# Half sequences 5 and 7 of a fused attention and FFN kernel: three rounds of scores in one burst, their fourth round in the next one's first burst, and later steps in a new order

## The chip, the cores and the metric

The kernel runs on one core of one Trainium2 chip. The metric is the device time of one execution in microseconds (us). Three runs of the kernel before took 229.24, 229.81 and 229.96 us; their median is 229.81. The profile is of one further execution.

## What is computed

An attention over 4 batches, 8 heads, 768 positions and 64 values per head is followed by an FFN over all 3072 tokens. Heads 0, 2 and 6 see every earlier position ("retrieval"); the other five see the first 4 positions and the last 64. The reference, cut:

```python
scores = scale * np.matmul(q, k.transpose(0, 1, 3, 2))
causal = rel >= 0
stream_keep = causal & (is_sink | in_win)          # 4 sinks, window of 64
mask = np.where(retr, causal, stream_keep)         # per head
a = softmax(np.where(mask, scores, -1e9))
x = np.matmul(a, v).transpose(0, 2, 1, 3).reshape(B * S, H * D)    # 3072 x 512
h = x @ w_in                                       # 512 -> 2048
g = h * (1.0 / (1.0 + np.exp(-beta * h)))
out = g @ w_out                                    # 2048 -> 512
```

## The kernel before

The 3072 tokens are eight *half sequences* (units) n = 0 to 7 of 384 queries: n = 2b + u is half u of batch b. The title counts them from one, so its fifth and seventh are n = 4 and n = 6, first halves. For each unit the kernel does, in this order:

- load q, k and v from HBM on the queue of the SP engine (`wf`), cast q and k to bf16 on GpSimd (`c`), and turn them with DMA transposes into `QK` (SP's queue too);
- copy pieces that the matmuls want side by side: `KP` and `QD` (the latter written into `k2f`), and for the values `vs`, `vz`, `VE` (from `vf`) beside `vb`;
- scores, on TensorE, in *rounds*: round (pi, ri) is round ri of head pair pi. A round writes one double bank of PSUM (`sp`, there are two) or, if `lent` says so, two of the four single banks (`b`). Rounds stand together in *bursts* (`BURSTS`, chosen by `kind_of(n)`). The exponentials of a round (`exps`, ScalarE, into `es`) free its banks, then its masks follow on VectorE;
- `pv`: exponentials times values into `sp`, and the sums of the exponentials into a bank; the sums go over `sc`, `rec` and `rd` (DMAs of a few KB and a reciprocal) and come back spread over the partitions as `R`; VectorE multiplies `sp` by `R` into `xT`, the FFN's input, and this frees `sp`;
- the FFN: 16 steps of four 128x384 matmuls with `w_in`, a tanh each on ScalarE (`t`) and the gate product on VectorE (`gT`); then 48 matmuls of 128x512 with `w_out` (in steps of three), a copy `osb` and a store.

TensorE (PE) works on 128x128 tiles in the FFN, on 64x64 or 64x128 tiles in the scores, 128x64 in `pv` and 128x32 in the sums. While one unit's FFN runs, the next units' attention stands between its steps.

Nothing is scheduled when it runs. Each step is declared with its engine or engines, what it needs and gives, and the buffers it takes and drops. The list `SEQUENCE` then says in which order all 1109 steps are written out, `CHOICE` the engine of those that may stand on several, and `SLOTS` the bank for each step that takes one. Every engine executes its own steps in that order. All instructions go through one recording helper, so that they all carry line L123.

In the scores of n = 4 and 6 the matmuls of a burst are handed out in turn to four 64x64 quadrants of the array (`scores_mixed`), which then work side by side.

Of the kernel before, what the change touches and what calls it, by code (L numbers as in the profile page):

```python
# [20 lines left out]
W = 64  # L21
# [71 lines left out]
]  # L93
CHOICE = (
    "daagaddadadddadaddaddgggdgdddgaaaggggggaaagdddaddaddagddddgaaddgddaaadagddadadagggggadggagdgggagggdd"
    "gaadaaadaaadaaadaadaadaaaada"
# [3 lines left out]
    "0301100101201013021302130210130211031001201032100123012301230123001200131230120130123012310021013203"  # L100
    "01130012103210013201320132100023102301231212310231001230123012301230210"
# [71 lines left out]
def kernel(  # L173
# [478 lines left out]
    def wide(pi, ri, n):  # L652
# [13 lines left out]
    def lent(pi, ri, n):  # L666
        return packed(n) and n % 2 and (pi, ri) in LENT
# [20 lines left out]
    def scores(x, pi, ri, mixed=None):  # L688
# [22 lines left out]
        for i, half in enumerate(rounds[ri]):  # L711
# [8 lines left out]
            for (kind, h, kb, col, q0, n) in half:  # L720
# [22 lines left out]
                else:  # L743
# [5 lines left out]
                    m = W if pi == 3 or (packed(x.n) and (ri > 1 or not u)) or ri == 4 else 128  # L749
# [722 lines left out]
```

## Time and profile before

| | |
|---|---|
| median of three runs | 229.81 us (229.24 to 229.96) |
| the profiled execution | 228.85 us |
| its span | 227.1 us |
| TensorE busy | 220.0 us, 2595 matmuls |
| VectorE busy | 152.0 us, 391 instructions |
| ScalarE busy | 144.4 us, 244 instructions |
| GpSimd busy | 97.1 us, 238 instructions |
| granted TensorE clock, mean | 0.999 |
| moved by DMA | 42.28 MB, mean 186 GB/s |

The span goes from the first to the last record of the trace; the time of the same execution holds 1.75 us more. Times of single instructions are from the profiled execution alone, which was 0.96 us shorter than the median. A matmul's length reaches into the next one in the rows, so distances between matmuls are taken from start to start.

### The profile page before, as it was taken

How to read it: one execution, taken by the hardware profiler on the slowest of the kernel's cores; microseconds unless marked ns; L12 is line 12 of the kernel's file. 1: busy time of each engine (PE TensorE's matmuls, PEld its weight loads, DVE VectorE, ACT ScalarE, POOL GpSimd, SP SyncE). 2: the span in 40 equal slices, each digit the busy share in tenths (PEclk: the TensorE clock that was granted, in tenths of full speed). 3: DMA queues.
4: the chain of work that ended last, by engine and by line, in shares of the span. 5: the costliest groups of instructions: out<-in, count | busy, mean ns of one | idle time of the engine just before them, and what ended most of it. 6: DMA issues, size and time to landing. Idle time of an engine off the chain costs nothing.

```text
span 227.1 us, 6564 instructions
## 1 busy us (share of the span) xinstructions
PE 220.0 (97%) x2595; PEld 127.2 (56%) x2595; DVE 152.0 (67%) x391; ACT 144.4 (64%) x244; POOL 97.1 (43%) x238
## 2 busy tenths in 40 slices
PE   7688999999999999999999999999999999999995
PEld 7564567664545565555654665465655555456543
DVE  5787988888292878856862668983796864157700
ACT  6899979886447488616786198318965665118620
POOL 5528966965978108749566293042800000000000
PEclk9999999999999999999999999999999999999999
DMA  6999999998999969999999996947801027021012
GB/s 185 283 321 369 242 343 349 371 335 217 233 205 244 213 131 235 270 176 208 267 219 189 202 214 192 219 26 178 188 0 46 4 89 200 3 92 46 3 46 92
DMA packets 84264, 42.28 MB, mean 186 GB/s; under 512 B 66042, under 2 KB 77002, under 8 KB 84234
## 3 DMA queue, kind: packets, MB, share of 16 engines
q1 hardware_dynamic: 83962, 41.67, 76.7%
q8 instruction: 20, 0.33, 0.6%
q10 hardware_dynamic: 272, 0.20, 0.3%
q14 instruction: 10, 0.08, 0.1%
HBM read 32.27 MB, written 6.37 MB: 170 GB/s over the span
## 4 chain that ended last, share of the span: by engine, by line
PE 87%; DMA 5%; DVE 3%; ACT 2%; SPq 1%; issue 1%; POOL 0%; ACTq 0%
PE b L123 77%; PE sp L123 10%; DMA vf<-in_v_dram 3%; DMA q2f<-in_q_dram 2%; DVE gT L123 1%; ACT t L123 1%; SPq L123 1%; ACT R L123 1%; DVE vs L123 1%; DVE xT L123 0%; ACT vb L123 0%; DVE QK L123 0%; POOL c L123 0%; DVE b L123 0%; DVE lo L123 0%
## 5 line engine op out<-in xcount | busy, mean ns | idle before, releaser
L123 PE MATMUL b<-xT,w_in 128*128 128x384 bf16 x512 | 89.9, 326 | 0.1
L123 PE MATMUL b<-w_out,gT 128*128 128x512 bf16 (+2 forms) x400 | 88.3, 371 | 0.0
L123 DVE SCALAR_TENSOR_TENSOR gT<-t,b 128x384 bf16<-128x384 f32 x128 | 68.5, 551 | 26.2 <-ACT t L123 22.5
L123 ACT ACTIVATE t<-b,beta_h 128x384 f32<-128x384 f32 x128 | 72.2, 586 | 18.3 <-PE b L123 9.7
L123 PEld LDWEIGHTS <-w_in 128*128 128x128 bf16 x512 | 48.6, 98 | 33.4 <-issue 0.6
L123 PEld LDWEIGHTS <-gT 128*128 128x128 bf16 x400 | 37.4, 98 | 40.9 <-issue 0.8
L123 ACT ACTIVATE es<-sp 128x1024 bf16<-128x1024 f32 (+2 forms) x44 | 41.2, 961 | 6.5 <-PE sp L123 6.0
L123 ACT ACTIVATE osb<-b 128x512 f32<-128x512 f32 (+1 forms) x18 | 10.5, 583 | 34.7 <-PE b L123 34.7
L123 DVE TENSOR_TENSOR xT<-sp,R 64x384 bf16<-64x384 f32 (+4 forms) x31 | 16.6, 554 | 12.2 <-PE sp L123 9.2
L123 POOL CAST c<-wf 128x256 bf16<-128x256 f32 x48 | 20.7, 473 | 7.6 <-DMA wf<-in_k_dram 7.4
L123 POOL COPY KP<-QK 128x24 bf16<-128x24 bf16 (+5 forms) x41 | 9.9, 286 | 27.1 <-DMA QK<-c 16.6
L123 PE MATMUL sp<-QK 64*64 64x128 bf16 (+6 forms) x360 | 14.9, 240 | 0.9 <-ACT QK L123 0.8
L123 DVE TENSOR_TENSOR es<-es,mask_s 128x128 bf16<-128x128 bf16 (+8 forms) x34 | 13.0, 402 | 3.8 <-ACT es L123 3.6
L123 PEld LDWEIGHTS <-QK 64*64 64x64 bf16 (+1 forms) x432 | 10.8, 106 | 7.2 <-issue 4.9
L123 DVE TENSOR_TENSOR es<-es,mask_c 128x128 bf16<-128x128 bf16 (+3 forms) x42 | 10.4, 272 | 6.2 <-ACT es L123 6.1
L123 POOL CAST vb<-wf 128x512 bf16<-128x512 f32 x18 | 11.2, 629 | 7.9 <-DMA wf<-in_v_dram 7.8
L123 PE MATMUL sp<-es,vb 128*64 128x64 bf16 (+5 forms) x245 | 13.0, 233 | 0.3 <-ACT es L123 0.3
L123 ACT COPY sc<-b 128x384 f32<-128x384 f32 x5 | 2.4, 479 | 15.7 <-PE b L123 15.7
L123 DVE TENSOR_SCALAR osb<-b 128x512 f32<-128x512 f32 (+1 forms) x7 | 4.7, 667 | 11.3 <-PE b L123 11.3
L123 PEld LDWEIGHTS <-vb 128*64 128x64 bf16 x257 | 11.6, 111 | 0.7 <-issue 0.3
L123 POOL CAST w_in<-wf 128x512 bf16<-128x512 f32 x16 | 9.4, 624 | 4.7 <-DMA wf<-in_moe_w_in_dram 4.6
L123 DVE COPY QK<-b 128x384 bf16<-128x384 bf16 (+1 forms) x13 | 8.2, 640 | 4.8 <-PE b L123 4.7
(120 smaller groups left out, 212.1 us busy)
## 6 DMA issues: line engine op xcount, KB each, us to landing
out_dram<-osb SPq DMA_DIRECT2D x23, 256.0 KB, 3.6
wf<-in_v_dram SPq DMA_DIRECT2D x18, 256.0 KB, 5.3
wf<-in_moe_w_in_dram SPq DMA_DIRECT2D x4, 1024.0 KB, 8.5
wf<-in_moe_w_out_dram SPq DMA_DIRECT2D x4, 1024.0 KB
R<-rd SPq DMA_DIRECT2D x9, 384.0 KB, 5.7
q2f<-in_q_dram SPq DMA_DIRECT2D x16, 192.0 KB, 4.1
wf<-in_q_dram SPq DMA_DIRECT2D x12, 256.0 KB, 4.0
wf<-in_k_dram SPq DMA_DIRECT2D x12, 256.0 KB, 3.8
```

What stands on the lines that cost most here:

```text
L123: ins = f(*a, **k)
```

## The change

For n = 4 and 6 the two bursts of two rounds become one burst of three rounds: (3,0), (0,0) and (0,1). Pair 3's rounds of these units write two single banks instead of a double bank. The round left over, (3,1), joins the first burst of the next unit (n = 5 and 7), which becomes (0,0), (0,1) and the other unit's (3,1). That burst is handed out to quadrants by `scores_mixed` as well, and its eight 64x128 matmuls are written as sixteen of 64x64. `scores_mixed` and the steps for exponentials and masks take the unit's number with each round.

There are two steps fewer, so every step behind them has a number that is lower by two. `SEQUENCE`, `CHOICE` and `SLOTS` are the same, but for these numbers, up to the first burst of n = 4. From there on the order, the banks, and the engine of some copies are new: the `vs` copies of n = 4 (two), one of n = 5 and one of n = 7, and the nine `KP` copies of n = 6 go from GpSimd to VectorE, one `vs` copy of n = 5 and one of n = 6 from VectorE to GpSimd, and eight output copies change between ScalarE and VectorE.

```diff
-    0, 2, 467, 477, 482, 478, 14, 12, 484, 4, 6, 483, 485, 8, 486, 464, 1, 3, 470, 80, 469, 28, 82, 26, 29, 27, 10,
...
+    0, 2, 465, 475, 480, 476, 14, 12, 482, 4, 6, 481, 483, 8, 484, 462, 1, 3, 468, 80, 467, 28, 82, 26, 29, 27, 10,
...
     BURSTS = [
         [[(0, 0), (0, 1)], [(3, 0), (3, 1)]],
         [[(0, 0), (0, 1)], [(1, 0), (0, 2), (3, 0)], [(2, 0), (0, 3), (3, 1)]],
-        [[(0, 0), (3, 0)], [(0, 1), (3, 1)]],
+        [[(3, 0), (0, 0), (0, 1)]],
     ]
 
     LENT = {(1, 0), (2, 0)}
 
     def lent(pi, ri, n):
+        if n in (4, 6):
+            return pi == 3
         return packed(n) and n % 2 and (pi, ri) in LENT
 
...
-                    m = W if pi == 3 or (packed(x.n) and (ri > 1 or not u)) or ri == 4 else 128
+                    m = W if pi == 3 or (packed(x.n) and (ri > 1 or not u or x.n > 4)) or ri == 4 else 128
...
-    def scores_mixed(x, bu):
+    def scores_mixed(bu):
 
         todo = []
-        for pi, ri in bu:
-            scores(x, pi, ri, todo)
+        for n, pi, ri in bu:
+            scores(units[n], pi, ri, todo)
...
-    BURST_COST = [[0.465, 0.48], [0.445, 0.7, 0.7], [0.465, 0.48]]
+    BURST_COST = [[0.465, 0.48], [0.445, 0.7, 0.7], [0.7]]
...
-        rounds = [(pi, ri) for bu in bursts for (pi, ri) in bu]
+        rounds = [(pi, ri) for bu in bursts for (pi, ri) in bu] + ([(3, 1)] if n in (4, 6) else [])
         for bi, bu in enumerate(bursts):
             needs, take, gives, drop, cost = [], [], [], [], 0.0
+            bu = [(n, pi, ri) for (pi, ri) in bu] + ([(n - 1, 3, 1)] if n in (5, 7) and not bi else [])
-            for (pi, ri) in bu:
+            for (m, pi, ri) in bu:
+                u, first_half = m % 2, m - m % 2
...
-                take += [("b", (n, pi, ri, i), 1) for i in range(2)] if lent(pi, ri, n) else [("sp", (n, pi, ri), 1)]
+                take += [("b", (m, pi, ri, i), 1) for i in range(2)] if lent(pi, ri, m) else [("sp", (m, pi, ri), 1)]
...
-            cost = cost if early else BURST_COST[kind_of(n)][bi]
+            cost = cost if early else 0.7 if len(bu) > 2 else BURST_COST[kind_of(n)][bi]
-            add("pe", cost, lambda bu=bu: scores_mixed(x, bu) if kind_of(n) == 2 else [scores(x, pi, ri) for (pi, ri) in bu],
+            add("pe", cost, lambda bu=bu: scores_mixed(bu) if kind_of(n) == 2 or any(w[0] != n for w in bu) else [scores(x, pi, ri) for (_, pi, ri) in bu],
...
-                add("act", exp_cost(pi, ri, n), lambda pi=pi, ri=ri: exps(x, pi, ri),
+                add("act", exp_cost(pi, ri, m), lambda m=m, pi=pi, ri=ri: exps(units[m], pi, ri),
-                    drop=[("b", (n, pi, ri, i)) for i in range(2)] if lent(pi, ri, n) else [("sp", (n, pi, ri))])
+                    drop=[("b", (m, pi, ri, i)) for i in range(2)] if lent(pi, ri, m) else [("sp", (m, pi, ri))])
```

The first place is TensorE ahead of the first burst of n = 5. In the rows, `w_out` and `w_in` are FFN matmuls, and `QK_109` is the transposed q and k of n = 5; brackets hold the semaphores that an instruction waits for. Before:

```order
L123 MATMUL b_2448<-w_out_125,gT 128x512
L123 LDWEIGHTS w_in_114 [waits DVE_49]
L123 MATMUL b_2462<-xT,w_in_114 128x384 [waits Activation_49]
L123 LDWEIGHTS w_in_114
L123 MATMUL b_2462<-xT,w_in_114 128x384 [waits DVE_49]
L123 LDWEIGHTS w_in_114
L123 MATMUL b_2462<-xT,w_in_114 128x384 [waits DVE_49]
L123 LDWEIGHTS w_in_114
L123 MATMUL b_2462<-xT,w_in_114 128x384 [waits DVE_49]
L123 LDWEIGHTS QK_109 [waits DMAHW7_49,DMAHW6_49,DMAHW5_49]
L123 MATMUL sp_2481<-QK_109 128x384 [waits PE_49]
```

After:

```order
L123 MATMUL b_2374<-w_out_124,gT 128x512
L123 LDWEIGHTS gT
L123 MATMUL b_2374<-w_out_125,gT 128x512
L123 LDWEIGHTS QK_109 [waits DMAHW6_49,DMAHW7_49,DMAHW5_49,DVE_49]
L123 MATMUL sp_2386<-QK_109 64x384 [waits PE_49]
L123 LDWEIGHTS QK_109
L123 MATMUL sp_2386<-QK_109 64x384
```

The step with `w_in` (four matmuls of n = 3) no longer stands between the `w_out` step and the burst, and the burst's first weight load waits for VectorE as well as for the three transposes. Further ahead, not shown, stand one burst of n = 4 where two were, and the sums of n = 3 have gone behind the burst.

The second place is SP's queue of DMAs ahead of the transposes `QK_109` of n = 5. `R`, `rd` and `q2f` belong to the sums of n = 3, `wf` with `in_k` is the load of n = 5's k, `vf` a small load of v for n = 4's `VE`, and `out` a store. Before:

```order
L123 DMA rd<-rec 96x32
L123 DMA wf<-in_k_dram 128x8x64 x3
L123 DMA out_dram<-osb 128x512 x2
L123 DMA R<-rd 64x2x384 x2
L123 DMA R<-rd 64x1536
L123 DMA q2f<-rd 64x128
L123 DMA vf<-in_v_dram 10x8x64 x3
L123 DMA_TRANSPOSE QK_109<-c 128x8x128 x3
```

After:

```order
L123 DMA out_dram<-osb 128x512
L123 DMA vf<-in_v_dram 10x8x64 x3
L123 DMA rd<-rec 96x32
L123 DMA wf<-in_k_dram 128x8x64 x3
L123 DMA R<-rd 64x2x384 x2
L123 DMA R<-rd 64x1536
L123 DMA q2f<-rd 64x128
L123 DMA_TRANSPOSE QK_109<-c 128x8x128 x3
```

The three `vf` loads stood behind `R` and `q2f` and now stand ahead of `rd`, the `in_k` loads and `R`. The transposes have the same transfers ahead of them as before, but for where the stores stand.

The third place is VectorE at the multiplies of n = 4 (`xT<-sp,R`), ahead of the first burst of n = 6, whose q and k are `QK_110`. Before:

```order
L123 TENSOR_TENSOR xT<-sp_2859,R 64x384 x2
L123 TENSOR_TENSOR xT<-sp_2859,R 128x384
L123 COPY vs<-vb 64x1536
L123 TENSOR_TENSOR xT<-sp_2882,R 128x768
L123 COPY k2f<-QK_110 64x128
L123 COPY k2f<-QK_110 64x256
L123 SCALAR_TENSOR_TENSOR gT<-t,b_2984 128x384
```

After:

```order
L123 TENSOR_TENSOR xT<-sp_2886,R 64x384 x2
L123 TENSOR_TENSOR xT<-sp_2886,R 128x384
L123 COPY vs<-vb 64x1536
L123 TENSOR_TENSOR xT<-sp_2859,R 128x768
L123 COPY vs<-vb 4x3x448
L123 COPY vb<-vb 4x12x64
L123 COPY vb<-vb 4x3x64
L123 COPY k2f<-QK_110 64x128
L123 COPY k2f<-QK_110 64x256
L123 COPY KP_111<-QK_110 128x5x60
L123 COPY KP_111<-QK_110 128x5x4
L123 COPY KP_111<-QK_110 128x6x4
```

Between the multiplies and the `k2f` copies now stand three copies of the values (`vs`, `vb`), and the `KP` copies of n = 6 (nine, of which three are shown) follow them, ahead of the gate products.

More of the change, by code (lines that the diff above doesn't have):

```diff
@@ L41 @@
 SEQUENCE = [
[51 rows of a table removed]
[51 rows of a table added]
 ]
 CHOICE = (
-    "daagaddadadddadaddaddgggdgdddgaaaggggggaaagdddaddaddagddddgaaddgddaaadagddadadagggggadggagdgggagggdd"
-    "gaadaaadaaadaaadaadaadaaaada"
+    "daagaddadadddadaddaddgggdgdddgaaaggggggaaagdddaddaddagddddgaaddgddaaadagddadadaddgggagdgaggggdadggdd"
+    "gaadaaadaadddaaaadaddaaaaada"
 )
@@ L99 @@
     "0120130120131210031201100312010312132301201031210032103101230012031203120312310231010210310210231021"
-    "0301100101201013021302130210130211031001201032100123012301230123001200131230120130123012310021013203"
-    "01130012103210013201320132100023102301231212310231001230123012301230210"
+    "0301100101201013021302130213021300121001031213001120312031203120321013100120301210321032103210301210"
+    "103203101013200113201320132130102031200132013201320131021032103210321032013"
 )
@@ L1245, in attention @@
         bursts = BURSTS[kind_of(n)] if not early else [[(pi, ri)] for pi in range(NP) for ri in range(len(rounds_of(pi, n)))]
-        rounds = [(pi, ri) for bu in bursts for (pi, ri) in bu]
+        rounds = [(pi, ri) for bu in bursts for (pi, ri) in bu] + ([(3, 1)] if n in (4, 6) else [])
         for bi, bu in enumerate(bursts):
             needs, take, gives, drop, cost = [], [], [], [], 0.0
-            for (pi, ri) in bu:
-                needs += [("QK", n, pi, 0), ("QK", n, pi, 1)] + ([("QK", first_half, pi, 1)] if u else [])
-                if any(h is not None and h[0][0] == "k" for h in rounds_of(pi, n)[ri]):
-                    needs += [("KS", 0, p) for p in range(1, NP)] + [("QK", n, p, 0) for p in range(1, NP)]
+            bu = [(n, pi, ri) for (pi, ri) in bu] + ([(n - 1, 3, 1)] if n in (5, 7) and not bi else [])
+            for (m, pi, ri) in bu:
+                u, first_half = m % 2, m - m % 2
+                needs += [("QK", m, pi, 0), ("QK", m, pi, 1)] + ([("QK", first_half, pi, 1)] if u else [])
+                if any(h is not None and h[0][0] == "k" for h in rounds_of(pi, m)[ri]):
+                    needs += [("KS", 0, p) for p in range(1, NP)] + [("QK", m, p, 0) for p in range(1, NP)]
                     drop.append(("KP3", "c"))
@@ L1256, in attention @@
                         take.append(("KP1", "k", 3))
-                if packed(n) and not u:
-                    needs += [("QK", n, p, i) for p in ((0, 3) if (pi, ri) == (0, 0) else (0, 1, 2) if (pi, ri) == (3, 0) else (0, 1, 2, 3)) for i in range(2)]
-                    needs += [("KP", n, p) for p in ((), (1, 2), (1, 2, 3))[pi and 1 + ri]]
-                    needs += ([("S", n, 0, 1)] if kind_of(n) == 0 else []) if pi else [("QD", n)]
+                if packed(m) and not u:
+                    needs += [("QK", m, p, i) for p in ((0, 3) if (pi, ri) == (0, 0) else (0, 1, 2) if (pi, ri) == (3, 0) else (0, 1, 2, 3)) for i in range(2)]
+                    needs += [("KP", m, p) for p in ((), (1, 2), (1, 2, 3))[pi and 1 + ri]]
+                    needs += ([("S", m, 0, 1)] if kind_of(m) == 0 else []) if pi else [("QD", m)]
@@ L1261, in attention @@
                     if (pi, ri) == (0, 0):
-                        drop.append(("k2f", (n, "d")))
+                        drop.append(("k2f", (m, "d")))
                     if (pi, ri) == (3, 1):
-                        drop += [(f"KP{p}", n) for p in (1, 2, 3)]
-                        gives += [("sc", n, 1), ("sc", n, 2)]
-                if packed(n) and u and pi and ri == 0:
-                    needs.append(("KP", n, pi))
-                    drop += [] if pi == 3 else [(f"KP{pi}", n)]
@@ L1269, in attention @@
-                if packed(n) and u and (pi, ri) in ((1, 0), (0, 3)):
-                    needs += [("QK", m, 3, i) for m in (n, first_half) for i in range(2)] + [("KP", n, 3)]
-                    drop += [("KP3", n)] if pi == 0 else []
-                if packed(n) and u and pi == 3:
-                    needs.append(("QD", n))
-                    drop += [("k2f", (n, "d"))] if ri else []
-                take += [("b", (n, pi, ri, i), 1) for i in range(2)] if lent(pi, ri, n) else [("sp", (n, pi, ri), 1)]
@@ L1276, in attention @@
-                if ri and (pi, ri - 1) not in bu:
-                    needs.append(("S", n, pi, ri - 1))
+                        drop += [(f"KP{p}", m) for p in (1, 2, 3)]
+                        gives += [("sc", m, 1), ("sc", m, 2)]
+                if packed(m) and u and pi and ri == 0:
+                    needs.append(("KP", m, pi))
+                    drop += [] if pi == 3 else [(f"KP{pi}", m)]
+                if packed(m) and u and (pi, ri) in ((1, 0), (0, 3)):
+                    needs += [("QK", w, 3, i) for w in (m, first_half) for i in range(2)] + [("KP", m, 3)]
+                    drop += [("KP3", m)] if pi == 0 else []
@@ L1278, in attention @@
+                if packed(m) and u and pi == 3:
+                    needs.append(("QD", m))
+                    drop += [("k2f", (m, "d"))] if ri else []
+                take += [("b", (m, pi, ri, i), 1) for i in range(2)] if lent(pi, ri, m) else [("sp", (m, pi, ri), 1)]
+                if ri and (m, pi, ri - 1) not in bu:
+                    needs.append(("S", m, pi, ri - 1))
                 if ri == 0:
-                    take.append((*es_ring(pi, n), 3 if packed(n) and (pi < 2 or not u) else 2))
@@ L1280, in attention @@
-                gives.append(("S", n, pi, ri))
-                if ri == len(rounds_of(pi, n)) - 1:
-                    gives.append(("sc", n, pi))
+                    take.append((*es_ring(pi, m), 3 if packed(m) and (pi < 2 or not u) else 2))
+                gives.append(("S", m, pi, ri))
+                if ri == len(rounds_of(pi, m)) - 1:
+                    gives.append(("sc", m, pi))
                 cost += 0.335 if pi == 3 and ri in (1, 2) else 0.195
-            cost = cost if early else BURST_COST[kind_of(n)][bi]
@@ L1285, in attention @@
-            add("pe", cost, lambda bu=bu: scores_mixed(x, bu) if kind_of(n) == 2 else [scores(x, pi, ri) for (pi, ri) in bu],
-                needs=needs, gives=gives, take=take, drop=drop, mode=("qk", "sum") if any(h is not None and h[0][0] == "k" for h in rounds_of(*bu[-1][:1], n)[bu[-1][1]]) else "qk")
-            for j, (pi, ri) in enumerate(bu):
-                add("act", exp_cost(pi, ri, n), lambda pi=pi, ri=ri: exps(x, pi, ri),
-                    needs=[("S", n, pi, ri)], gives=[("E", n, pi, ri)],
-                    drop=[("b", (n, pi, ri, i)) for i in range(2)] if lent(pi, ri, n) else [("sp", (n, pi, ri))])
-                c = mask_cost(pi, ri, n)
+            cost = cost if early else 0.7 if len(bu) > 2 else BURST_COST[kind_of(n)][bi]
@@ new lines, in attention @@
+            add("pe", cost, lambda bu=bu: scores_mixed(bu) if kind_of(n) == 2 or any(w[0] != n for w in bu) else [scores(x, pi, ri) for (_, pi, ri) in bu],
+                needs=needs, gives=gives, take=take, drop=drop, mode=("qk", "sum") if any(h is not None and h[0][0] == "k" for h in rounds_of(bu[-1][1], n)[bu[-1][2]]) else "qk")
+            for (m, pi, ri) in bu:
+                add("act", exp_cost(pi, ri, m), lambda m=m, pi=pi, ri=ri: exps(units[m], pi, ri),
+                    needs=[("S", m, pi, ri)], gives=[("E", m, pi, ri)],
+                    drop=[("b", (m, pi, ri, i)) for i in range(2)] if lent(pi, ri, m) else [("sp", (m, pi, ri))])
+                c = mask_cost(pi, ri, m)
@@ L1292, in attention @@
                 if c:
                     add(("dve", "pool") if early else "dve", (c, 0.1 + 2.5 * (c - 0.07)) if early else c,
-                        lambda e="dve", pi=pi, ri=ri: masks(x, pi, ri, ENG[e]), port=True,
-                        needs=[("E", n, pi, ri), ("const", "m") if all(t[0][0] == "c" for t in masks_of(pi, ri, n)) else ("const", "mask" if n < 2 else "new", u)],
-                        gives=[("M", n, pi, ri)])
+                        lambda e="dve", m=m, pi=pi, ri=ri: masks(units[m], pi, ri, ENG[e]), port=True,
@@ L1297, in attention @@
+                        needs=[("E", m, pi, ri), ("const", "m") if all(t[0][0] == "c" for t in masks_of(pi, ri, m)) else ("const", "mask" if m < 2 else "new", m % 2)],
+                        gives=[("M", m, pi, ri)])
+        u, first_half = x.u, n - x.u
         M = [("M" if mask_cost(pi, ri, n) else "E", n, pi, ri) for (pi, ri) in rounds]
```

100 rows, old and new, of the table SEQUENCE are left out of this document.

## The prediction

> **What bounds the kernel now.** I read the page first: the busy times, the chain that ended last, the groups.
>
> ```profile
> span 227.1 us, 6564 instructions
> PE 220.0 (97%) x2595; PEld 127.2 (56%) x2595; DVE 152.0 (67%) x391; ACT 144.4 (64%) x244; POOL 97.1 (43%) x238
> PE 87%; DMA 5%; DVE 3%; ACT 2%; SPq 1%; issue 1%; POOL 0%; ACTq 0%
> ...
> L123 PEld LDWEIGHTS <-QK 64*64 64x64 bf16 (+1 forms) x432 | 10.8, 106 | 7.2 <-issue 4.9
> ```
>
> TensorE (PE) is busy for 97% of the span and is 87% of the chain. Next I asked for the busy time in the part that the change orders anew (by column: the stretch, its length, the busy time and instructions of PE, its weight loads, VectorE, ScalarE and GpSimd, the granted clock, the DMA share, GB/s).
>
> ```profile
> 88.00:200.00 112.00, 112.00 (x1288) 62.49 (x1287) 73.72 (x177) 66.84 (x110) 40.94 (x100) 1.00 0.75 154
> ```
>
> From 88 to 200 us PE is busy for all 112 us at full clock. So two things alone can move the time: what PE executes, and a wait that the new order brings where there is none now. An engine with spare time, or another engine for a copy, counts only as far as it makes PE wait. I then read PE's timeline around the bursts of scores (start, length, tiles out<-in, tile mode, shape, count).
>
> ```profile
> 85.77 2.28 PE L123 MATMUL b<-xT,w_in 128*128 128x384 bf16 x13
> 87.98 0.40 PE L123 MATMUL sp<-QK 64*64 64x320 bf16 x5
> ...
> 88.58 1.15 PE L123 MATMUL b<-xT,w_in 128*128 128x384 bf16 x6
> ...
> 91.93 0.38 PE L123 MATMUL sp<-QK 64*64 64x320 bf16 x8
> ...
> 92.60 0.60 PE L123 MATMUL b<-w_out,gT 128*128 128x512 bf16 x2
> ...
> 97.22 0.21 PE L123 MATMUL b<-es,one_z 128*32 128x64 bf16 x4
> ...
> 97.84 4.71 PE L123 MATMUL b<-w_out,gT 128*128 128x512 bf16 x21
> 103.13 0.61 PE L123 MATMUL sp<-QK 64*128 64x384 bf16 x8
> 103.67 0.82 PE L123 MATMUL b<-xT,w_in 128*128 128x384 bf16 x4
> 104.33 2.11 PE L123 MATMUL b<-w_out,gT 128*128 128x512 bf16 x9
> 106.37 0.22 PE L123 MATMUL b<-QK,KP 64*64 64x64 bf16 x2
> ...
> 107.19 8.62 PE L123 MATMUL b<-xT,w_in 128*128 128x384 bf16 x52
> ```
>
> Two prices follow. Four `w_in` matmuls take 104.33 - 103.67 = 0.66, so one is 0.163 us; 13 of them are 2.12, yet the burst behind the 13 starts 87.98 - 85.77 = 2.21 later: entering a burst costs 0.09 to 0.10 beyond the streaming, and I take the same for leaving it. Nine `w_out` matmuls and one such entry are 106.37 - 104.33 = 2.04, so one is 0.216. A burst's price is the distance from its first matmul to the next large one, and 0.10 for the entry: 0.70 for the first of n=4, 0.77 for its second, 0.64 for the first of n=5, 0.92 for the second of n=5 (50 matmuls).
>
> **Term 1: two bursts fewer.** Before, n=4 has two bursts and n=5's first follows: 0.70 + 0.77 + 0.64 = 2.11. After, the same rounds are two bursts, of 50 and 56 matmuls by the order. The nearest row is the 50-matmul burst at 106.37, so 0.92 for the one, and 0.96 for the other with six matmuls more: 1.88, a gain of 0.23. The other pair has the same form:
>
> ```profile
> 133.94 0.40 PE L123 MATMUL sp<-QK 64*64 64x320 bf16 x5
> ...
> 134.54 6.03 PE L123 MATMUL b<-xT,w_in 128*128 128x384 bf16 x36
> ...
> 140.50 0.42 PE L123 MATMUL sp<-QK 64*64 64x320 bf16 x14
> ...
> 141.15 0.82 PE L123 MATMUL b<-w_out,gT 128*128 128x512 bf16 x3
> ...
> 154.27 0.61 PE L123 MATMUL sp<-QK 64*128 64x384 bf16 x8
> 154.81 1.47 PE L123 MATMUL b<-w_out,gT 128*128 128x512 bf16 x6
> ```
>
> The first burst of n=6 is 0.70, the first of n=7 is 0.64, and for the second of n=6 141.15 - 140.50 + 0.10 = 0.75: together 2.09, a gain of 0.21. Term 1 is -0.44. Its ends: if the merged matmuls don't share the array any better than a small burst's do, each new burst is up to 1.0 and the gain is 0.2; if the four quadrants are kept full, some 0.83 each, and it is 0.8. Eight matmuls of 64x128 become sixteen of 64x64. The weight loads that come with them are 106 ns each in the page, but 50 of them pass in 0.82 us in the burst at 106.37, so they run side by side and I charge nothing. The Trainium skill, TensorEngine Tiling (Array Packing), section on restrictions, says that column tiling disables Fast Weight Load, which would speak against splitting these matmuls; were eight more loads serial at this trace's 106 ns, each pair would lose 0.8 us. The 0.82 us for 50 of them speaks against that here, and the sum goes without it.
>
> **Term 2: the first burst of n=5 comes before its data.** It needs the transposed QK of n=5 (DMA transposes on SP's queue) and both double banks, which the multiplies `xT<-sp,R` of n=3 free. In before these were ready shortly ahead of PE:
>
> ```profile
> 90.41 1.97 SPq L123 DMA_DIRECT2D R<-rd  x3
> 93.06 1.34 SPq L123 DMA_DIRECT2D vf<-in_v_dram  x3
> 94.51 4.92 SPq L123 DMA_TRANSPOSE QK<-c  x3
> 99.48 1.49 SPq L123 DMA_DIRECT2D out_dram<-osb  x1
> ...
> 98.31 2.83 DVE L123 TENSOR_TENSOR xT<-sp,R 64x384 bf16<-64x384 f32 x6 [2.55 <-DMA R<-rd]
> 101.18 0.29 DVE L123 TENSOR_TENSOR xT<-sp,q2f 64x128 bf16<-64x128 f32 x1
> 102.50 0.68 DVE L123 COPY k2f<-QK 64x384 bf16<-64x384 bf16 x2 [1.03 <-DMA QK<-c]
> ...
> 99.02 0.55 POOL L123 CAST VE<-vf 30x448 bf16<-30x448 f32 x1 [4.14 <-DMA vf<-in_v_dram]
> ```
>
> VectorE (DVE) stood idle for the last transpose and went on at 102.50. PE came at 103.13, 0.63 later: that is all the slack. The new order asks for the burst earlier. Ahead of it no longer stand 4 `w_in` matmuls (0.65) and the sums of n=3 (97.84 - 97.22 = 0.62), both of which now follow it, and one burst of n=4 takes the place of two (0.70 + 0.77 - 0.92 = 0.55); the 39 `w_out` matmuls ahead of it are as many as before. PE would come 1.82 earlier, at 101.3.
>
> The queue of SP before the three transposes holds the same transfers in both orders, in other places, and the transposes can't be issued sooner: they land at 102.5 again, a wait of 1.2. A second chain gives about as much: R of n=3 landed at 98.31 and its multiplies ended at 101.47. Three transfers `vf` (1.34 us of issue) now stand ahead of it, so it lands between 99.0, when those landed themselves, and 98.31 + 1.34 = 99.65; with 101.47 - 98.31 = 3.16 of multiplies the banks are free at 102.2 to 102.8. Both chains say 0.9 to 1.5; I take **+1.2**. Ends: 0.2, if the transposes land 1.0 sooner with the queue's other order, and 1.9, if DVE's other work falls between these multiplies or the transposes slip by as much on a queue that has no gap here. All of PE's work stands behind this wait; nothing of it can be made up, as PE has no idle time later.
>
> **Term 3: thin margins behind.** The nine copies KP of n=6 go from POOL to DVE, behind the multiplies of n=4.
>
> ```profile
> 48.19 1.12 DVE L123 COPY KP<-QK 128x300 bf16<-128x300 bf16 x9
> ...
> 127.35 2.76 PE L123 MATMUL b<-w_out,gT 128*128 128x512 bf16 x12
> ...
> 125.86 1.73 DVE L123 TENSOR_TENSOR xT<-sp,R 64x384 bf16<-64x384 f32 x3 [3.67 <-PE sp L123]
> 127.63 0.56 DVE L123 COPY vs<-vb 64x1536 bf16<-64x1536 bf16 x1
> 128.22 0.96 DVE L123 TENSOR_TENSOR xT<-sp,R 128x768 bf16<-128x768 f32 x1
> 129.20 0.60 DVE L123 COPY k2f<-QK 64x128 bf16<-64x128 bf16 x2
> ...
> 145.17 0.62 DVE L123 COPY vs<-vb 4x1344 bf16<-4x1344 bf16 x1
> 145.82 0.67 DVE L123 COPY vb<-vb 4x768 bf16<-4x768 bf16 x2
> ```
>
> In the new order DVE does 1.73 + 0.56 + 0.96 + 0.62 + 0.67 + 0.60 + 1.12 = 6.26 from the first multiply to the last KP copy. In the same time PE has the rest of `pv` and the sums (127.35 - 125.86 = 1.49 by the start of the `w_out` run behind them), 21 `w_out` (4.53), 4 `w_in` (0.65) and an entry: 6.77. The margin is 0.5, less if masks of n=5 hold DVE first. The `w_in` run of n=5 now has three masks in the middle of its gate products, which leaves as little. I take +0.15 for both together, ends 0 and 0.5. The other copies that change engines have margins of over a microsecond, and I cost them at nothing; the POOL work that goes is hidden by POOL's idle half.
>
> **The sum.** -0.44 + 1.2 + 0.15 = +0.91. The profiled execution took 228.85 us (span 227.1, 1.75 outside it), so 229.76 for its like. It lies 0.96 below the median of the runs, 229.81, to which the sum is added: 230.72, told as 230.7.
>
> **Rivals.** *The transposes come in time, no wait (the one that is not slower).* The new order lets three other transfers pass on SP; if the transposes land by 101.2 and R as well, only terms 1 and 3 are left: 229.81 - 0.44 + 0.15 = 229.5, within 0.3%. It decides at a landing of 101.3 in the new trace. Against it stand SP's rows: the issue of the three transposes ends where the next transfer begins, at 99.48, and the last landed 3.0 later. A transpose moves 128x8x128 values of two bytes, 256 KB, and its median is
>
> ```profile
> QK<-c SPq DMA_TRANSPOSE x12, 4.7
> ```
>
> 4.7 us from issue to landing. The Trainium skill, DMA: Bandwidth & Descriptors, section on latency and other measured facts, gives 0.6 us to the first byte and 261 GB/s for such a transpose, from which I estimate 1.6 us: by that the last would land near 99.8, PE would never wait, and this rival would be the forecast. The trace's 4.7 and the landing at 102.5 are nearly three times that, so it gets no more than 0.21.
>
> *A second wait at n=6's burst.* The sums' transfer of n=4 now stands ahead of n=6's loads on SP and waits for sums that PE does only behind n=5's first burst. If n=6's transposes land 2 us later than the 129.2 of the copies above, KP is ready at 129.2 + 2 + 0.60 + 1.12 = 132.9 0.9 to 1.1 behind PE, which comes at 101.3 + 57 `w_out` (12.31) + 68 `w_in` (11.08) + 6.0 of bursts, `pv` and sums in between = 130.7, and 131.9 with the first wait. In place of part of term 3 that is 0.7 more: 231.4. For it: SP stands behind one more wait. Against: the k loads of n=6 are now ahead of `rd`. Chance 0.14.
>
> *Full packing and no wait.* Term 1 at -0.8 and nothing else: 229.0, chance 0.08.
>
> **How the numbers follow.** The forecast has 0.57, its rivals 0.21, 0.14 and 0.08. About 0.3% (0.69 us) is what a measurement of this kernel can tell from no change. Slower by more: the second wait 0.14 and most of the forecast (0.51; with a wait under 1.0 us it falls within), 0.65. Within: 0.06 of the forecast and 0.19 of the first rival, 0.25. Faster: full packing 0.08, and 0.02 of the first rival with its gain at the upper end, 0.10. The range begins at 229.2, a little under the first rival with a better packing, and ends at 231.8, the forecast with -0.2, a wait of 1.7 and 0.5 behind it; full packing and a second wait on top of a long first one are left out.
>
> **What would show it.** In the new trace PE's timeline should have a gap of about 1.2 us ahead of n=5's first burst, released by a transpose or by `xT<-sp,R`, with the burst at 102.2 to 102.8; the two pairs of bursts should be 0.92 to 0.96 each; ahead of n=6's burst PE should be idle for less than 0.5. A burst of n=5 at 101.3 with no idle time before it refutes term 2, and a change of more than 1 us that lies in none of these places refutes the whole account.

## The result and the profile after

The changed kernel takes 232.68 us (median of 6 runs, 231.67 to 233.77) against 229.87 for the kernel before (6 runs beside it, 229.24 to 230.44): 1.0127 times as long, 95% interval 1.0093 to 1.0161. Runs more than 1.5% above the fastest of the same kernel are left out of all medians and ratios here and below. The forecast was 230.7 in a range from 229.2 to 231.8: the direction holds, but the change forecast, 0.9, is a third of the 2.8 that came. The profiled execution took 232.38, 3.53 more than that of before.

The page after (lines 2 to 4 as in the prediction; then two groups):

```profile
span 230.7 us, 6579 instructions
PE 218.6 (95%) x2589; PEld 127.8 (55%) x2611; DVE 158.6 (69%) x405; ACT 143.9 (62%) x246; POOL 91.4 (40%) x223
PE 67%; DMA 16%; POOL 5%; ACT 3%; SPq 3%; DVE 2%; issue 2%; ACTq 0%; POOLq 0%
...
L123 PE MATMUL b<-w_out,gT 128*128 128x512 bf16 (+2 forms) x378 | 84.4, 370 | 2.2 <-issue 1.6
...
L123 PEld LDWEIGHTS <-gT 128*128 128x128 bf16 x400 | 37.5, 98 | 40.8 <-issue 0.5
```

PE's share of the chain fell from 87% to 67%; DMAs have 16%. There are 378 `w_out` matmuls for 400 of their weight loads: 22 records are missing. Each missing one leaves the 0.22 of a matmul unaccounted for; the 1.6 us of "issue" below are ten of these and no time lost. The next view shows what PE waited for from 45 us on (what waited, for what: us in all, times, longest). In before it is empty.

```profile
PE b L123 <- DVE gT L123: 2.0, 2, 1.7
PE b L123 <- issue: 1.6, 10, 0.2
PE sp L123 <- DMA QK<-c: 1.1, 1, 1.1
```

PE's timeline at the bursts of n=5 (first, third), n=6 and n=7 (first), and at both ends of the stretch that I measure:

```profile
47.12 0.40 PE L123 MATMUL sp<-QK 64*64 64x320 bf16 x5
...
98.69 2.97 PE L123 MATMUL b<-w_out,gT 128*128 128x512 bf16 x13
102.73 0.63 PE L123 MATMUL sp<-QK 64*64 64x384 bf16 x16 [1.07 <-DMA QK<-c]
...
118.98 1.46 PE L123 MATMUL b<-w_out,gT 128*128 128x512 bf16 x6
...
123.60 0.59 PE L123 MATMUL b<-w_out,gT 128*128 128x512 bf16 x2 [0.16 <-issue]
...
134.29 0.29 PE L123 MATMUL b<-QK 64*64 64x256 bf16 x1
...
135.12 1.15 PE L123 MATMUL b<-xT,w_in 128*128 128x384 bf16 x6
...
154.55 0.63 PE L123 MATMUL sp<-QK 64*64 64x384 bf16 x16
...
155.41 0.82 PE L123 MATMUL b<-w_out,gT 128*128 128x512 bf16 x2
```

The new bursts are 135.12 - 134.29 + 0.10 = 0.93 and 155.41 - 154.55 + 0.10 = 0.96, and the first burst of n=5 starts at 102.73 after 1.1 of waiting. In this profile those two terms came as forecast. Most of the rest lies between 118.98 and 123.60. These 4.6 us hold six `w_out` matmuls (1.30), a burst with its entry and its end (0.9) and a missing record (0.2); the other 2.2 are waits.

What led up to these waits, on the chain that ended last (start, length, what):

```profile
111.08 5.21 DMA wf<-in_k_dram
116.33 0.08 issue
116.41 0.74 POOL c L123 x2
117.15 1.87 POOL vs L123 x3
119.04 2.57 DVE vb L123 x2
121.61 0.93 DVE gT L123 x2
122.54 0.04 issue
122.58 0.39 PE b L123 x25
```

and VectorE with the rows ahead of it:

```profile
112.33 0.35 DVE L123 RECIPROCAL rec<-rec 96x32 f32<-96x32 f32 x1 [0.62 <-DMA rec<-sc]
...
117.38 1.16 DVE L123 COPY vs<-vb 4x896 bf16<-4x896 bf16 x1
119.04 2.57 DVE L123 COPY vb<-vb 4x512 bf16<-4x512 bf16 x2 [0.50 <-POOL vs L123]
121.53 1.00 DVE L123 SCALAR_TENSOR_TENSOR gT<-t,b 128x384 bf16<-128x384 f32 x2
```

The three copies `vk` of n=6 (`vs<-vb` and `vb<-vb`) hold VectorE from 117.38 to 121.53, between two gate products. The second of them needs a `vs` copy that the change gave to GpSimd, where it stands behind casts of k of n=6, and these wait for a load. The gate products behind are late, and with them the two banks that n=5's third burst borrows.

Two things are new here. In before VectorE did that `vs` copy itself, and `vk` of n=6 stood right behind it and behind the masks of n=6, 30 us later than now (before; the first row holds the `vs` copy of 64x1536 and the first copy of `vk`):

```profile
147.01 0.95 DVE L123 COPY vs<-vb 64x1536 bf16<-64x1536 bf16 x2
147.98 0.39 DVE L123 COPY vb<-vb 4x512 bf16<-4x512 bf16 x2
```

The new order moved `vk` up, in among the gate products of n=3; the new `CHOICE` made it wait there for GpSimd.

VectorE also waits at the reciprocal of n=4 for a DMA of 12 KB. ScalarE copied these sums at 107.03, 9.1 us later than before:

```profile
97.96 0.48 ACT L123 COPY sc<-b 128x384 f32<-128x384 f32 x1 [2.40 <-PE b L123]
```

```profile
107.03 0.48 ACT L123 COPY sc<-b 128x384 f32<-128x384 f32 x1
```

(before, after.) The sums of n=4 need all its rounds, and the round (3,1) now stands in n=5's first burst. On SP the transfer then queues behind three loads of q that take 4.26 us there:

```profile
104.49 4.26 SPq L123 DMA_DIRECT2D wf<-in_q_dram  x3
108.85 0.73 SPq L123 DMA_DIRECT2D rec<-sc  x1
109.63 3.84 SPq L123 DMA_DIRECT2D wf<-in_k_dram  x3
```

### The profile page after: what moved, and what is told of

It is laid out like the page before. It is cut to its first block, busy times and chain, and to the rows that moved or that the text cites. A ratio compares the mean times of both kernels' runs of the same rounds, so it can differ in the third digit from the quotient of the medians.

```text
span 230.7 us, 6579 instructions
## 1 busy us (share of the span) xinstructions
PE 218.6 (95%) x2589; PEld 127.8 (55%) x2611; DVE 158.6 (69%) x405; ACT 143.9 (62%) x246; POOL 91.4 (40%) x223
## 4 chain that ended last, share of the span: by engine, by line
PE 67%; DMA 16%; POOL 5%; ACT 3%; SPq 3%; DVE 2%; issue 2%; ACTq 0%; POOLq 0%
PE b L123 61%; PE sp L123 6%; DMA wf<-in_k_dram 4%; DMA k2f<-in_k_dram 4%; DMA wf<-in_moe_w_in_dram 4%; SPq L123 3%; DMA QK<-c 3%; DMA q2f<-in_q_dram 2%; POOL w_in L123 2%; POOL c L123 1%; DVE vb L123 1%; DVE gT L123 1%; POOL vs L123 1%; ACT t L123 1%; ACT osb L123 1%
## 5 line engine op out<-in xcount | busy, mean ns | idle before, releaser
L123 PE MATMUL b<-xT,w_in 128*128 128x384 bf16 x512 | 88.9, 326 | 0.1
L123 PE MATMUL b<-w_out,gT 128*128 128x512 bf16 (+2 forms) x378 | 84.4, 370 | 2.2 <-issue 1.6
L123 ACT ACTIVATE es<-sp 128x1024 bf16<-128x1024 f32 (+2 forms) x40 | 37.1, 961 | 4.1 <-PE sp L123 3.7
L123 ACT ACTIVATE osb<-b 128x512 f32<-128x512 f32 (+1 forms) x16 | 9.2, 580 | 34.8 <-PE b L123 34.8
L123 POOL CAST c<-wf 128x256 bf16<-128x256 f32 x48 | 19.0, 436 | 12.0 <-DMA wf<-in_q_dram 8.3
L123 DVE TENSOR_TENSOR es<-es,mask_s 128x128 bf16<-128x128 bf16 (+8 forms) x34 | 14.3, 437 | 10.3 <-ACT es L123 10.1
L123 POOL COPY KP<-QK 128x24 bf16<-128x24 bf16 (+5 forms) x32 | 8.5, 306 | 30.0 <-PE b L123 17.9
L123 ACT ACTIVATE es<-b 128x432 bf16<-128x432 f32 (+3 forms) x20 | 9.9, 550 | 11.5 <-PE b L123 11.5
L123 PE MATMUL sp<-QK 64*64 64x128 bf16 (+7 forms) x318 | 13.7, 248 | 2.0 <-DMA QK<-c 1.1
L123 DVE TENSOR_SCALAR osb<-b 128x512 f32<-128x512 f32 (+1 forms) x9 | 6.1, 673 | 11.4 <-PE b L123 11.3
```

Source lines behind the costliest of these rows:

```text
L123: ins = f(*a, **k)
```

## The experiments

Each profile starts differently: the first burst, at 47.1 in before, comes as late as 48.9 in kernels whose order up to there is the same. (In five of the profiles the granted clock is 0.50 for 3.4 or 6.8 us between 7.7 and 14.6 us from the start.) So I compare the distance from that burst's start to the last matmul's start: 176.97 before, 180.50 after. The waits are what a distance between two matmuls has over that of the same two without a wait. The four new bursts cost 0.42 less than the six before: 2 x (0.93 + 0.96) for 2.11 + 2.09. Each distance is 176.97 - 0.42 + the waits of its row, within 0.3 but for `e_rec_late` (told there). Median and ratio are of several executions, distance and waits of one.

| kernel | median | ratio to before (95%) | distance | waits of PE behind 45 us: n=5's first burst; near 113; its third burst; elsewhere |
|---|---|---|---|---|
| after | 232.68 | 1.0127 (1.0093 to 1.0161) | 180.50 | 1.14; 0.20; 2.19; 0.39 |
| after_again | 232.96 | 1.0132 (1.0054 to 1.0210) | 179.22 | 0.14; 0.53; 1.85; 0.17 |
| a_vk6_late | 230.66 | 1.0049 (1.0018 to 1.0080) | 179.69 | 1.19; 1.72; 0; 0.17 |
| b_vs6_dve | 230.91 | 1.0051 (1.0020 to 1.0082) | 178.69 | 1.08; 0.62; 0; 0.44 |
| c_vef_late | 233.38 | 1.0145 (1.0098 to 1.0193) | 179.83 | 0; 1.61; 1.50; 0.17 |
| d_both | 231.57 | 1.0079 (1.0051 to 1.0107) | 179.63 | 0.87; 2.04; 0; 0.17 |
| e_rec_late | 233.92 | 1.0200 (1.0121 to 1.0279) | 181.66 | 0.78; 0; 2.43; 0.34 |
| f_rec_vk | 231.44 | 1.0059 (1.0025 to 1.0092) | 178.49 | 0.16; 0; 0; 1.65 |
| g_all | 231.63 | 1.0066 (1.0035 to 1.0096) | 179.57 | 1.09; 0; 0; 1.79 |
| h_all_out | 233.42 | 1.0168 (1.0114 to 1.0223) | 179.81 | 0; 0; 0; 3.19 |
| i_chain | 231.61 | 1.0086 (1.0056 to 1.0116) | 179.27 | 1.54; 0; 0; 1.19 |
| j_chain_all | 232.00 | 1.0113 (1.0051 to 1.0174) | 179.08 | 0.26; 0; 0; 2.00 |
| k_best | 231.51 | 1.0137 (1.0047 to 1.0227) | 177.20 | 0; 0; 0; 0.60 |

**`a_vk6_late`** moves step 390, `vk` of n=6, in `SEQUENCE` back to behind the masks of n=6, where it stands in before:

```diff
-    ... 803, 382, 378, 390, 750, 806, ...
+    ... 803, 382, 378, 750, 806, ...
+    ... 838, 401, 390, 842, ...
```

> The changed kernel, with one step moved: VectorE's three copies `vk` of n=6 (vs<-vb, vb<-vb) go from between the gate products 12 and 14 of n=3 to behind the masks of n=6. Theory: these copies wait there for a `vs` copy of n=6 that now stands on GpSimd, run beside GpSimd's copies, and so hold up the gate products whose banks the third burst of n=5 needs. Then the waits ahead of that burst (1.75 and 0.44 us in the changed kernel's profile) go and the time falls by 1.8 to 2.3 us to about 230.6. Rival (the gate products are late because ScalarE's tanh or exponentials are): those waits stay and the time stays at 232.7, within 0.4.

The median fell by 2.0 us, and the waits at n=5's third burst are gone. The profiled execution was one of its slowest (232.35) and shows two other waits, the first of which the profile after had at 0.2:

```profile
PE b L123 <- DVE gT L123: 1.6, 1, 1.6
PE sp L123 <- DVE xT L123: 1.1, 1, 1.1
```

The 1.6 lies at 115, the place that the table calls "near 113": VectorE stood 2.13 us at the reciprocal, for rec<-sc.

**`b_vs6_dve`** undoes the engine of one step (the letter for `vs` of n=6, first copy, in `CHOICE`):

```diff
-    vs, n=6, half 0: "g"
+    vs, n=6, half 0: "d"
```

> The changed kernel with one engine undone: the `vs` copy of n=6 (64 rows) runs on VectorE again, ahead of `vk` of n=6 at the same place. Theory 1 (what costs is that VectorE waits in order for a copy that GpSimd does late): vk takes about 1.0 us instead of 4.2, the waits ahead of n=5's third burst all but go, 230.5 to 231.0. Theory 2 (what costs is VectorE's copies running beside GpSimd's): the wait for GpSimd goes, but vk still takes over 2 us beside GpSimd's casts, and the time falls by less than 1 us, to 231.8 or more.

The time, 230.91, and the third burst without a wait agree with theory 1. `vk` took 0.47 and 1.12 here beside GpSimd's casts. In `a_vk6_late`, where GpSimd stands idle beside them, the same three copies took 0.38 and 0.39 (here, then there):

```profile
118.78 0.47 DVE L123 COPY vs<-vb 4x896 bf16<-4x896 bf16 x1
119.27 1.12 DVE L123 COPY vb<-vb 4x512 bf16<-4x512 bf16 x2
```

```profile
148.42 0.38 DVE L123 COPY vs<-vb 4x896 bf16<-4x896 bf16 x1
148.82 0.39 DVE L123 COPY vb<-vb 4x512 bf16<-4x512 bf16 x2
```

So of the 4.2 us in the changed kernel 0.8 are the copies' own, 0.5 the wait for GpSimd, and 2.9 stretching beside its work. Theory 2 has a share, then. What sets the stretch, 0.8 here and 2.9 there, wasn't told apart; the `vb<-vb` copies ran beside casts of v here (1.12), and beside casts of k and then of v in the two profiles of the changed kernel (2.57 and 2.56). The Trainium skill, Advanced Engine Details and Errata, section on VectorE performance modes, says that VectorE's second SBUF port is shared with GpSimd, so that GpSimd's instructions and VectorE's two-port ones block each other. These rows agree in direction; no run shows whether these copies use two ports.

Either edit alone ends the wait at the third burst. So it took both: `vk` early, and its `vs` copy on GpSimd.

**`c_vef_late`** and **`d_both`** take the three `vf` loads (step 301) from ahead of `rd` of n=3 (275 is its reciprocal) to behind n=5's transposes (332), and GpSimd's `VE` (302) behind `KP` (340); `d_both` has `vk` late as well:

```diff
-    ... 674, 703, 303, 301, 275, 710, ...
+    ... 674, 703, 303, 275, 710, ...
-    ... 709, 307, 332, 278, ...
+    ... 709, 307, 332, 301, 278, ...
```

> The changed kernel with the three small vf loads moved on SP from ahead of n=5's k loads to behind n=5's QK transposes (and the cast VE that waits for them behind KP of n=5 on GpSimd). Theory: the k loads, the R of n=3 and the transposes all come about 1.2 us earlier, so the wait of 1.1 us ahead of n=5's first burst goes: about 231.6. Rival 1 (the transposes are held by something else than the queue ahead): the burst still starts with a wait of over 0.7, 232.3 to 232.7. Rival 2 (the wait is given back by a new one at n=5's second burst, whose banks the exponentials free): the gap moves there, same time.

> Both moves together (vk of n=6 later, the vf loads behind the transposes). If the two waits are independent the gains add: 3.0 to 3.3 us less than the changed kernel, 229.4 to 229.7, which is 0.2 to 0.5 below the kernel before, about the gain of two bursts fewer (0.44). If one wait hides part of the other, or the earlier burst runs into n=6's loads, 230.0 to 230.8.

`c_vef_late` has no wait at n=5's first burst, but no gain: 1.61 near 113 (0.58 of it at 109, for a gate product that stood behind `vk` of n=4, whose `vb<-vb` copies took 1.18) and 1.50 at the third burst. `d_both` still waits 0.87 at the first burst, for `xT<-sp,R` (R came at 99.44), and 2.04 near 113. Its gain, 1.1, is less than that of moving `vk` alone, and the sum of two independent gains, 229.4 to 229.7, was missed. Both say that the wait near 113, small in the profile after, is a third one.

**`e_rec_late`, `f_rec_vk`, `g_all`, `h_all_out`** move the reciprocal of n=4 (315) and `rd` (316) later; `f` with `vk` late, `g` with the `vf` loads too, `h` with one store besides:

```diff
-    ... 373, 778, 315, 775, 389, 769, 316, 782, ... 784, 787, 379, 723, 797, ...
+    ... 373, 778, 775, 389, 769, 782, ... 784, 315, 787, 379, 723, 316, 797, ...
```

> The changed kernel with the reciprocal `rec` of n=4 moved on VectorE from between the gate products 4 and 5 of n=3 to behind product 8 (2.5 us later), and SP's `rd` that needs it moved behind the v loads of n=5 and a store. Theory: in the runs with another step moved, VectorE stood 0.8 to 2.5 us at this reciprocal for the tiny DMA rec<-sc, which now comes 9 us later than before because n=4's sums wait for the round in n=5's first burst; PE then stood 0.4 to 2.0 us at 113 for the bank. With the reciprocal later this wait goes; the wait at n=5's third burst stays or grows. 231.4 to 232.4, and no PE gap near 113. Rival (PE's gap near 113 comes from ScalarE or a slot, not from this DMA): the gap stays, 232.4 to 233.

> Reciprocal of n=4 later, and `vk` of n=6 later as well. Theory: of the waits only that ahead of n=5's first burst is left (about 1.1), so 229.87 - 0.42 + 1.1 + 0.1 to 0.4 of small ones = 230.7 (230.3 to 231.0). Rival (the time so won is lost again at n=6's first burst, since R of n=4 and the transposes of n=6 come later): a PE gap at 131 to 134 of a microsecond, 231.2 or more.

> All three moves: reciprocal of n=4 later, `vk` of n=6 later, the vf loads behind n=5's transposes. If the three waits are all that was lost: 229.4 to 229.9, within 0.2% of the kernel before. Where the first burst of n=5 still waits for R of n=3 (0.9 us in the profile of the two-step run), 230.2 to 230.6.

> The same, and one more transfer (an output store, 0.8 us of SP) moved from ahead of `rd` of n=3 and of n=5's k loads to behind n=5's transposes. Theory (SP's queue ahead of R and of the transposes sets the wait of n=5's first burst): that wait falls by a further 0.5 to 0.8 us and is under 0.4; 229.3 to 229.8. Rival (the landing of the DMAs doesn't follow SP's queue here): the wait stays where the kernel without this move has it.

The wait near 113 is gone in all four, so the reciprocal was its cause. The profiles where it stood early say the same by size. VectorE waited for rec<-sc, and PE behind it:

| profile | VectorE at the reciprocal | PE near 113, behind it |
|---|---|---|
| after | 0.62 | 0.20 |
| b_vs6_dve | 0.78 | 0.36 |
| after_again | 0.94 | 0.53 |
| c_vef_late | 1.45 | 1.03 |
| a_vk6_late | 2.13 | 1.72 |
| d_both | 2.46 | 2.04 |

(`b_vs6_dve` has 0.25 more at 117.5 in the first table, `c_vef_late` 0.58 more at 109.) PE lost VectorE's wait less 0.41 or 0.42 each time: that is all the slack of the order there.

The times miss: three of the four wait about 1 to 3 us at 130 instead, as the rival of `f_rec_vk` had it in kind. There R of n=4, issued later for the late `rd`, keeps the multiplies of n=4 (`f_rec_vk`, VectorE, then PE):

```profile
127.79 1.73 DVE L123 TENSOR_TENSOR xT<-sp,R 64x384 bf16<-64x384 f32 x3 [3.42 <-DMA R<-rd]
```

```profile
130.90 0.48 PE L123 MATMUL b<-xT,w_in 128*128 128x384 bf16 x2 [1.00 <-DVE xT L123]
```

With one store less ahead on SP, `h_all_out` has no wait at the first burst, where `g_all` has 1.09. This pair alone doesn't show that the queue sets the wait, as the changed kernel itself had 1.14 and 0.14 in two executions and `f_rec_vk` came to 0.16 without any of these moves. But the kernels below with the same store late have 0.26 or less in all their four profiles. `e_rec_late` holds 1.5 us more than its waits explain; its stretches around the third burst say why (columns as in the prediction: the stretch, its length, the busy time and instructions of PE, its weight loads, VectorE, ScalarE and GpSimd, the granted clock, the DMA share, GB/s):

```profile
119.40:122.80 3.40, 1.20 (x50) 0.88 (x48) 3.36 (x7) 0.58 (x1) 2.15 (x5) 1.00 0.41 83
122.80:126.20 3.40, 3.40 (x17) 1.32 (x10) 1.97 (x7) 2.75 (x4) 0.00 (x0) 0.53 1.14 193
```

After 3.4 us in which PE was busy for 1.2, the granted clock is 0.53 for the next 3.4.

**`i_chain`, `j_chain_all`** let the way of n=4's sums be short again: `rd` and R go ahead of v's loads of n=5 (333) and a store (723) on SP, the reciprocal three products later; `vk` of n=6 late; the last `vs` and `vk` of n=5 (338, 339) among the products of n=4. `j` has the `vf` loads and the store of `h` late too:

```diff
 SP:
 L123 DMA rd<-rec 96x32
-L123 DMA wf<-in_v_dram 128x8x64 x3
-L123 DMA out_dram<-osb 128x512
 L123 DMA R<-rd 64x4x384 x2
 L123 DMA_TRANSPOSE QK_110<-c 128x8x128 x3
+L123 DMA out_dram<-osb 128x512
+L123 DMA wf<-in_v_dram 128x8x64 x3
```

> The changed kernel with the way of n=4's sums made short again behind the point where they now start: on SP `rd` and `R` of n=4 go ahead of the v loads of n=5 and one store (3 us of SP), which follow n=6's transposes; on VectorE the reciprocal stands three products later, `vk` of n=6 behind n=6's masks, and the last `vs` and `vk` of n=5 among the gate products of n=4. Theory: the waits are all of one chain (sums of n=4, made 9 us later by the new burst, DMA, reciprocal, DMA, R, multiplies of n=4) and of vk of n=6. With both taken away only the wait ahead of n=5's first burst (0.2 to 1.1) is left: 229.7 to 230.6, no PE gap over 0.3 near 113, 122 and 130. Rival (every such move gives its time back at another DMA): a new PE gap of about 1 us at 130 to 148, 231.2 or more.

> The same, and the vf loads and one store moved behind n=5's transposes as well, which took the wait ahead of n=5's first burst away in the run before. Theory: no wait is left but small ones, so the two bursts fewer show: 229.73 - 0.42 + 0 to 0.4 = 229.3 to 229.7, at or just under the kernel before. Rival as for the other kernel: 230.5 or more, with a PE gap of about 1 us that is not in either place.

The waits near 113, at the third burst and at 130 for R are gone together in these two profiles, as the theory says. In their place PE waits 0.9 and 1.2 at 143 to 144, where I had put `vk` of n=5 (1.4 us of VectorE) between two gate products: my own edit's price. `i_chain` waits 1.54 at the first burst. The times missed and fell where the rivals had them, 231.2 and 230.5 or more.

**`k_best`** is `j_chain_all` with `vk` of n=5 behind the last products of n=4 and the reciprocal of n=5 two products later:

```diff
 VectorE: g(n=4,9)
-vk(n=5)
 ... g(n=4,14)
+vk(n=5)
 g(n=4,15), masks of n=6
```

> The kernel with the short way of n=4's sums and the vf loads and a store behind n=5's transposes, with two places mended at which its profile showed PE waiting for gate products of n=4: `vk` of n=5 goes to the end of those products (ahead of n=6's masks), the reciprocal of n=5 two products later. Theory (no wait over 0.3 us is left in PE's row): 229.3 to 229.9, same as the kernel before or up to 0.2% under it. Rival (the DMAs land so much later in some executions that other waits of a microsecond come in their place): 230.3 or more, and a wider spread of times than the kernel before has (2 us).

**`after_again`** is the changed kernel, not edited:

> The changed kernel once more, nothing edited, for a second profile. Theory (its three waits hang on DMA landings, so they change from one execution to the next while PE's own work does not): the burst of n=5 waits 0.5 to 1.5 again, the wait at 113 (0.2 before) and that at n=5's third burst (2.2 before) have other sizes, their sum with the rest between 2.5 and 4.5; 232 to 233.5. Rival (the waits are set by the order alone): each is the same within 0.2 us.

Its waits are 0.14 at n=5's first burst (1.14 in the first profile; 0.5 to 1.5 were expected), 0.53 near 113 (0.20) and 1.85 at the third burst (2.19), 2.7 in all. So the rival fails: the order alone doesn't set their size, though two of the three moved by only 0.3.

The profiled execution of `k_best`, 229.87, has one wait over 0.2, at n=7's first burst (0.42), and the distance 177.20, 0.23 over before's. Its median, 231.51, doesn't follow: 1.0137 times before, from 1.0047 to 1.0227. Two more profiles of it and of before:

> The kernel with every wait mended, once more, for another profile. Theory: in executions at 231 us and more PE waits 1 to 3 us in the second half (from 95 to 155 us) at steps that hang on a DMA landing; the distance from the first burst at 47 to the last matmul (177.2 in its first profile) is then 178 to 180. Rival (the spread is in the first 45 us, common to all kernels): that distance stays at 177.2 within 0.3 and the first burst comes later than 48.5.

> The same kernel, a third profile; expected as for the second one.

> The kernel before, unedited, a second profile. Theory: its order has room for late DMAs, so the distance from the first burst to the last matmul is 177.0 within 0.3 again, whatever the time, and its spread of 2 us lies ahead of the first burst. Rival: it has waits of 0.5 us or more behind the first burst in slower executions too.

> The kernel before, a third profile; expected as for its second one.

What PE waited for behind 45 us, in the second profile of `k_best` (231.13 us, distance 178.61), its third (230.87, 178.45), and the third of before (231.11, 177.89; the second, at 229.00, has no wait and 177.04):

```profile
PE sp L123 <- DMA QK<-c: 0.5, 1, 0.5
PE b L123 <- DVE gT L123: 0.4, 1, 0.4
PE b L123 <- DVE xT L123: 0.3, 1, 0.3
```

```profile
PE sp L123 <- DMA QK<-c: 0.6, 1, 0.6
PE b L123 <- ACT osb L123: 0.4, 1, 0.4
```

```profile
PE b L123 <- DVE gT L123: 0.7, 1, 0.7
```

So the mended order still waits 1.5 to 2 us in some executions, as its theory had it, each time at steps that hang on a DMA, above all n=7's first burst, the twin of n=5's. One of them is the reciprocal of n=4 again, three products later by now (second profile, VectorE):

```profile
113.63 0.35 DVE L123 RECIPROCAL rec<-rec 96x32 f32<-96x32 f32 x1 [0.96 <-DMA rec<-sc]
```

PE lost 0.55 behind it. Before waited once in three, 0.88, for a gate product that stood behind copies waiting for a transpose; there the rival held, and not the theory that its order has room for late DMAs. What the executions of `k_best` at 232 to 235 us wait for has no profile and stays open. No version beat the kernel before.

## Why the prediction was wrong

- **Two bursts fewer, -0.44: right.** New bursts of 0.93 and 0.96, for the forecast's 0.92 and 0.96, which makes -0.42.
- **The wait at n=5's first burst, +1.2: right in mechanism, and in size in one of two executions** (1.14 and 0.14 in the two profiles of the changed kernel, 0 to 1.54 elsewhere). It was one number for something that changes by 1 us between executions. Transposes and `xT<-sp,R` ended it in turn. Of six kernels with the loads ahead moved away four lost all or most of it (0, 0, 0.26, 0) and two kept it (0.87, 1.09), where R came late. The rival without this wait nearly got its condition in the second profile, but not its time (231.69), as the waits that it left out were there too. In the first profile the last transpose landed at 102.59, 3.15 us after its issue began at 99.44. The Trainium skill, DMA: Bandwidth & Descriptors, section on latency and other measured facts, gives 0.6 us to the first byte and 261 GB/s, by which the prediction's estimate was 1.6 us; the trace doesn't agree.
- **Term 3, +0.15: right where it looked, but it looked in the wrong places.** PE didn't wait at n=6's burst in either profile of the changed kernel, and lost 0.17 in n=5's run in both.
- **The step that failed** is the sentence "The other copies that change engines have margins of over a microsecond, and I cost them at nothing". One of them, `vs` of n=6, put VectorE's `vk` behind GpSimd's casts and a load, between gate products: 2.19 and 1.85 us. The sentence looks at engines alone. `vk` kept its engine and went 30 us up in VectorE's order, and the sum has no term for that at all. Undoing the engine alone gave 1.8 us back, moving `vk` back alone 2.0. The wait is 0 in every profile with either undone, and 1.50 to 2.43 in the four with neither (after, after_again, `c_vef_late`, `e_rec_late`).
- **The second rival had the right cause and the wrong place.** It saw that n=4's sums now come behind n=5's first burst and priced what SP then does to n=6's burst. The price was at the reciprocal, a step in the order of VectorE, 0.20 and 0.53 in the changed kernel and 0.36 to 2.04 in four others. I had followed SP's queue behind that transfer, and not the engine that waits for it.

With these the first profile closes: -0.42 + 1.14 + 0.20 + 2.19 + 0.39 (elsewhere) = 3.50, for a measured distance that is 3.53 longer.

## What to carry to other kernels

In an order with little slack, list every step that changes its place, not only those that change their engine. Price each by who stands behind it on its engine and on the engine that waits for it, not by the idle share of either: where VectorE stood at a reciprocal in front of gate products, the bound engine lost all of that wait but 0.42. Merging work across units delays whatever needs the earlier unit to be complete (here the sums, by 9 us); follow that chain to its end before counting the saved bursts. Once one such wait is mended, look for the next one in a profile rather than adding gains up: most of my sums missed that way.

## What the hardware showed that I had not expected

- A stretch of 3.4 us with PE busy for 35% was followed by 3.4 us at a granted clock of 0.53, so that a wait of 2.4 us cost 1.5 more (`e_rec_late`). The changed kernel's wait of 2.2 in the same place left PE busy for 48% of its stretch (119.00 to 122.40) and cost no clock; where the limit lies isn't shown. The Trainium skill, TensorE: Matmul & The Clock Gate, Part 1, has half rate after an idle window of about 3.4 us; here PE wasn't idle for all of it.
- The same two VectorE copies took 0.39 us with GpSimd idle, and 1.12 and 2.57 beside its casts.
- The same wait for the same transfers, in the same kernel, was 1.14 us in one execution and 0.14 in another.
